# A filter's first layer run as two 64-row tiles of TensorE instead of one 128-row product

## The chip, the cores and the metric

The kernel runs on one core of a Trainium2 chip. The time is that of one execution on the device in microseconds (us), from the first to the last instruction and what lies around them; less is better. One execution was also profiled: its span, its instructions and their waits are what the rows further down are taken from.

## The reference

A long convolution with a filter made by a small network is multiplied into the input, and its result goes through a soft mixture of experts. The change touches only the filter:

```python
def _attn_ref(x, v, pos_emb, w1, w2):          # x, v: (4, 11456, 128); pos_emb: (11456, 64)
    h_mlp = np.maximum(pos_emb @ w1, 0.0) @ w2  # w1: (64, 64), w2: (64, 128)
    window = np.exp(-0.01 * pos)[:, None]
    h_filt = h_mlp * window
    u = x * v
    ...                                         # y: causal convolution of u with h_filt
    return x * y

def _moe_ref(x, phi, w1, w2):
    ...                                         # softmax over tokens and over 32 slots, 8 experts
```

All numbers are 32-bit floats.

## The kernel before

The convolution is done by Fourier transforms of 197 x 111 points that are written as matrix products. The 11,456 positions are indexed by j (99 values, the partitions of most tiles here) and r (56 values, called rows here). Positions 111 j + r and 111 j - r are kept side by side, one for each sign: `pos` holds for each of the 56 rows a block of 128 x 99, in which partitions 0 to 63 are the 64 features of the positions of one sign and partitions 64 to 127 those of the other.

The program starts with the filter's first layer, `hid_step` and `hid_scale`. For each row r, one product (line L150) has the 128 x 99 block of `pos` as the stationary operand and `w1r[:, r]` as the moving one. `w1` is fed as a 128 x 128 matrix with the 64 x 64 weights in two diagonal blocks and zeros elsewhere, so that the 128 columns that come out are the 64 hidden units of the one sign and the 64 of the other. The factor of the window that depends on r is multiplied into `w1` ahead of the product: `w1r[:, r]` is a scaled copy of all 128 columns, made on ScalarE (`scale_one`, L120) for some rows and on POOL (`scale_many`, L123) for the others, three steps ahead. A 32-bit product is two instruction records of TensorE, each with a weight load (PEld) and a stream of the columns (PE).

The rows go in ten steps: 4, then five times 8, then 4, 4, 2 and 2. They are numbered 0 to 9 here, so step 0 is rows 0 to 3, step 1 rows 4 to 11, and step 5 rows 36 to 43. For a step, TensorE writes the products to a PSUM tile `ph` (four buffers), ScalarE writes the positive part of one sign to `hb` (L153), and two operations of VectorE (L155) take the positive part of the other sign and write sum and difference to `hid`. Before the first step eight products on zeros keep TensorE at work (`idle_products`, L117), and four more follow the last.

`pos` is loaded on SyncE's queue in pieces of 4, 4 and six times 8 rows (L288), behind them the inputs x and v of the convolution and the table W. Then follow, on TensorE, the first transform of `hid` (`filter_first`, L196), the second, which reads W (`filter_second`, L208), the first transform of the input (L174), and further on the filter's last layer (`filter_last`, L218: two products side by side in row halves 0 to 63 and 64 to 127) with the long middle part. VectorE prepares x and v meanwhile (L268 to L274). The order on each engine is the order in which the program is written (`inorder`).

Two other places serve as measures below. L707, in the part on experts, transposes 64 x 128 blocks in two row halves with 64 columns streamed. L886 is a single product there that streams one column.

Of the kernel before, what the change touches and what calls it, by code (L numbers as in the profile page):

```python
# [11 lines left out]
F32 = mybir.dt.float32  # L12
F32R = mybir.dt.float32r
AF = mybir.ActivationFunctionType
ALU = mybir.AluOpType
AX = mybir.AxisListType

B, S, D = 4, 11456, 128
# [3 lines left out]
J = 99  # L22
# [3 lines left out]
R = 56  # L26
RP = 64
FO = 64
# [20 lines left out]
@with_exitstack  # L49
def conv_gate_moe(ctx: ExitStack, tc: tile.TileContext, xf, vf, xi, xe, pos, w1, w2, win,  # L50
                  t1x, t1h, wt, t3, t4, phi, mw1, mw2, rep, out):
    nc = tc.nc
    dram = ctx.enter_context(tc.tile_pool(name="dram", bufs=1, space=bass.MemoryType.DRAM))
    hs = dram.tile([G - 1, HP, J, 2 * CG], F32, tag="hs", name="hs")
    scr = dram.tile([D * TOK], F32, tag="scr", name="scr")
    cp = ctx.enter_context(tc.tile_pool(name="cp", bufs=1))
    moe = Moe(tc, cp, scr, phi, mw1, mw2, rep, out)
    moe.ctx = ctx
    with ExitStack() as cctx:
        conv_part(cctx, tc, cp, moe, xf, vf, xi, xe, pos, w1, w2, win, t1x, t1h, wt, t3, t4, hs, scr)  # L60
    next(moe.steps, None)


def conv_part(ctx, tc, cp, moe, xf, vf, xi, xe, pos, w1, w2, win, t1x, t1h, wt, t3, t4, hs, scr):
    nc = tc.nc
# [3 lines left out]
    psh = hid_ps.enter_context(tc.tile_pool(name="psh", bufs=4, space=bass.MemoryType.PSUM))  # L69
# [9 lines left out]
    Tall = cp.tile([128, (B + 1) * 2 * CG * J], F32, tag="T", name="T")  # L79
# [4 lines left out]
    inorder = tc.keep_in_program_order  # L84
# [7 lines left out]
    hid = moe.E[:J, : 2 * RP * FO].rearrange("p (s r f) -> p s r f", s=2, r=RP)  # L92
# [4 lines left out]
    ring = moe.E[:, J * N1 : J * N1 + 2 * HK * 2 * D]  # L97
    ring = ring.rearrange("p (t g k x) -> p t g k x", t=2, g=G, k=HK)
    small = moe.E[:, J * N1 + 2 * HK * 2 * D :]
    w1s = small[:, : 2 * FO]  # L100
    w2s = small[:, 2 * FO : 2 * FO + D]
    wins = small[:, 2 * FO + D :][:, :R]
    tab1h = small[:J, 2 * FO + D + R :][:, : 4 * J]
    w1r = Tall[:, : R * 2 * FO].rearrange("p (r x) -> p r x", r=R)
    pt = W.rearrange("p k n -> p (k n)")[:, J * (N1 - R) :].rearrange("p (r j) -> p r j", r=R)
    spare = [moe.E[:, 4 * C * R + PW * i :][:, :PW] for i in range(2)]

    HR = 8
# [12 lines left out]

    def scale_many(r0, r1):
        inorder(nc.gpsimd.tensor_tensor(  # L123
            out=w1r[:, r0:r1], in0=w1s.unsqueeze(1).to_broadcast([128, r1 - r0, 2 * FO]), op=ALU.mult,
            in1=wins[:, r0:r1].unsqueeze(2).to_broadcast([128, r1 - r0, 2 * FO])))

    def hid_scale(i):
        r0, n = steps[i]
        if i == 0:
            for r in range(1, n):  # L130
                scale_one(r)
        elif i == 1:
            scale_many(r0, r0 + 4)
            for r in range(r0 + 4, r0 + n):
                scale_one(r)
        else:
            if n == HR:
                for r in range(r0 + n - 2, r0 + n):
                    scale_one(r)
                n -= 2  # L140
            if n == 2:
                scale_one(r0 + 1)
                n = 1
            scale_many(r0, r0 + n)

    def hid_step(r0, n):
        ph = psh.tile([J, HR, 2, FO], F32, tag="ph", name=f"ph_{r0}")
        for k in range(n):
            r = r0 + k
            inorder(nc.tensor.matmul(ph[:, k].rearrange("p h f -> p (h f)"), lhsT=pt[:, r],  # L150
                                     rhs=w1r[:, r] if r else w1s, start=True, stop=True))
        hb = ld.tile([J, HR, FO], F32, tag="lv", name=f"hb_{r0}", bufs=2)
        inorder(nc.scalar.activation(hb[:, :n], ph[:, :n, 0], AF.Relu))  # L153
        for s, op in enumerate((ALU.add, ALU.subtract)):
            inorder(nc.vector.scalar_tensor_tensor(out=hid[:, s, r0 : r0 + n], in0=ph[:, :n, 1], scalar=0.0,  # L155
                                                   op0=ALU.max, op1=op, in1=hb[:, :n]))

    def banks(g, u, name, large):
# [127 lines left out]
    for i, n in enumerate(loads):  # L286
        r0 = sum(loads[:i])
# [4 lines left out]
    for i, (r0, n) in enumerate(steps):  # L292
        hid_step(r0, n)
        if i + 3 < len(steps):
            hid_scale(i + 3)
# [878 lines left out]
    return dict(rep=rep, t1x=t1x, t1h=t1h, wt=wt, t3=t3, t4=t4, win=win)  # L1174


def _twice(a):
    o = np.zeros((2, a.shape[0], 2, a.shape[1]), a.dtype)
    o[0, :, 0] = o[1, :, 1] = a
    return o.reshape(2 * a.shape[0], -1)  # L1180


def _index(base):
    j = np.arange(-(JT // 2), JT // 2 + 1) if base else np.arange(J)
    r = np.arange(R)
    p = N1 * j[:, None] + r[None] + base
    b = N1 * j[:, None] - r[None] + base
    m = -N1 * j[:, None] - r[None] + base
    return p, b, m
# [99 lines left out]
```

## Time and profile before

| | |
|---|---|
| median of 3 runs | 890.41 us (890.39 to 890.75) |
| span of the profiled execution | 888.78 us |
| TensorE busy in that span | 858.3 us, 97% |
| first layer's products | 4.64 to 18.16 us |
| next layer's first product | 19.45 us |

The profiled execution is one execution, and its span runs from its first to its last instruction. Engines are PE (TensorE's products), PEld (its weight loads), DVE (VectorE), ACT (ScalarE), POOL (GpSimd) and SP (SyncE, which here only issues transfers). An arrow in brackets names the engine, tile and line whose end released the instruction after an idle time; "issue" there means that the profile shows nothing the engine waited for.

### The profile page before, as it was taken

To read this page: it belongs to the slowest core of one execution; us is meant where nothing else is said; L and a number is where in the kernel's file an instruction comes from. 1 tells how busy PE (TensorE), PEld (TensorE's weight loads), DVE (VectorE), ACT (ScalarE), POOL (GpSimd) and SP (SyncE) were. 2 spreads that over 40 slices of the span, in tenths; PEclk is the share of its full clock that TensorE was granted. 3 is DMA by queue.
4 is the path that set the end of the run, shared out by engine and by line. 5 is a ranking of instruction groups with operands and counts; after the bars stand their busy time and mean duration, and the time that the engine had idled before them with its cause. 6 is when DMAs were issued, how large, how long until landed. Compare 5 with 4: busy or idle time off the path is not lost. (4 is left out here: it accounts for less than half of the span.)

```text
span 888.8 us, 37282 instructions
## 1 busy us (share of the span) xinstructions
PE 858.3 (97%) x16192; PEld 792.5 (89%) x16192; DVE 714.9 (80%) x1239; ACT 455.9 (51%) x971; POOL 393.3 (44%) x538
## 2 busy tenths in 40 slices
PE   9999999999999999999999999999999999999991
PEld 9998989999999999999999999999999997666540
DVE  5967976898899889988988998899779148886791
ACT  5775558315811751473167128414821637887761
POOL 5003860492088029405910960393079013785750
PEclk9999999999999999999999999999999999999996
DMA  9963685548647755775386476557715979993698
GB/s 329 396 193 117 205 249 148 157 147 269 203 125 210 234 165 141 227 235 167 110 282 201 123 224 207 167 167 238 224 57 166 264 182 374 412 369 121 278 417 364
DMA packets 94386, 197.01 MB, mean 222 GB/s; under 512 B 14330, under 2 KB 55708, under 8 KB 90383
## 3 DMA queue, kind: packets, MB, share of 16 engines
q1 hardware_dynamic: 94046, 194.50, 66.8%
q8 instruction: 127, 2.08, 0.9%
q14 instruction: 37, 0.30, 0.1%
q10 hardware_dynamic: 144, 0.07, 0.0%
q0 software_dynamic: 32, 0.07, 0.0%
HBM read 137.73 MB, written 56.86 MB: 219 GB/s over the span
## 5 line engine op out<-in xcount | busy, mean ns | idle before, releaser
L350 POOL TENSOR_TENSOR T<-m 111x256 f32<-111x256 f32 (+1 forms) x199 | 150.8, 758 | 344.5 <-DVE m L344 344.5
L344 DVE TENSOR_TENSOR m<-p,T 111x1024 f32<-111x1024 f32 (+1 forms) x175 | 200.4, 1206 | 14.4 <-PE p L340 7.0
L360 PE MATMUL p<-tab,T 111*99 111x112 f32 x2048 | 205.4, 260 | 1.5 <-POOL T L351 0.3
L360 PEld LDWEIGHTS p<-tab,T 111*99 111x99 f32 x2048 | 198.8, 170 | 6.5 <-issue 1.6
L340 PE MATMUL p<-T,W 128*64 128x128 f32 (+1 forms) x3168 | 196.7, 276 | 0.4 <-issue 0.3
L420 ACT ACTIVATE vc<-p 128x416 f32<-128x416 f32 x112 | 51.9, 516 | 266.2 <-PE p L411 226.6
L340 PEld LDWEIGHTS p<-T,W 128*64 128x64 f32 (+1 forms) x3168 | 181.8, 127 | 2.7 <-issue 0.9
L411 PE MATMUL p<-tab,E 99*64 99x104 f32 x3584 | 174.1, 252 | 1.1 <-DVE E L373 0.6
L411 PEld LDWEIGHTS p<-tab,E 99*64 99x64 f32 x3584 | 166.4, 136 | 3.1 <-ACT vc L420 0.8
L375 ACT ACTIVATE E<-p 99x448 f32<-99x448 f32 x254 | 132.2, 577 | 63.7 <-PE p L360 57.5
L351 POOL TENSOR_TENSOR T<-m 111x256 f32<-111x256 f32 (+1 forms) x199 | 147.4, 740 | 0.0
L186 ACT ACTIVATE T<-p 128x396 f32<-128x396 f32 x240 | 100.4, 539 | 11.5 <-PE p L174 11.4
L174 PE MATMUL p<-tab1x,x 53*64 53x99 f32 x3648 | 86.7, 246 | 0.2 <-ACT E L224 0.2
L174 PEld LDWEIGHTS p<-tab1x,x 53*64 53x64 f32 x3648 | 79.8, 132 | 4.4 <-ACT E L224 0.4
L436 DVE TENSOR_TENSOR p<-p,vc 128x832 f32<-128x832 f32 x46 | 47.3, 1028 | 10.3 <-ACT vc L420 10.3
L268 DVE TENSOR_TENSOR x<-x,T 128x448 f32<-128x448 f32 x51 | 31.6, 619 | 22.2 <-PE p L174 11.2
L274 DVE TENSOR_TENSOR x<-T 128x224 f32<-128x224 f32 x102 | 39.2, 426 | 1.8
L270 DVE TENSOR_TENSOR T<-x 128x224 f32<-128x224 f32 x102 | 39.2, 425 | 1.7
L224 ACT ACTIVATE E<-fl 111x512 f32<-111x512 f32 (+1 forms) x50 | 26.9, 629 | 21.3 <-PE fl L218 21.3
L444 DVE TENSOR_TENSOR E<-p,E 128x824 f32<-128x824 f32 x36 | 36.6, 1017 | 1.2
L713 ACT ACTIVATE xreg<-pt 128x512 f32<-128x512 f32 (+1 forms) x68 | 35.0, 612 | 0.8 <-PE pt L707 0.7
L344 DVE TENSOR_TENSOR m<-p,E 111x1024 f32<-111x1024 f32 (+1 forms) x25 | 28.7, 1202 | 5.1 <-PE p L340 4.9
(156 smaller groups left out, 972.8 us busy)
## 6 DMA issues: line engine op xcount, KB each, us to landing
x<-in_xf_dram SPq DMA_DIRECT2D x114, 256.0 KB, 4.2
out_dram<-xreg SPq DMA_DIRECT2D x16, 1024.0 KB, 10.5
E<-in_xi_dram SPq DMA_DIRECT2D x37, 412.0 KB, 4.0
T<-in_vf_dram SPq DMA_DIRECT2D x65, 224.0 KB, 5.0
scr<-E SPq DMA_DIRECT2D x67, 206.0 KB, 3.7
T<-hs SPq DMA_DIRECT2D x63, 154.0 KB, 4.5
hs<-E SPq DMA_DIRECT2D x12, 784.0 KB, 4.6
mv<-in_vf_dram SPq DMA_DIRECT2D x42, 224.0 KB, 5.2
```

The source lines that it names most:

```text
L174: inorder(nc.tensor.matmul(ps[h][RP * d : RP * d + RP, i, s, :], lhsT=sd[js, i, s, d, :], rhs=tab1x[js, J * (s + d) : J * (s + d + 1)], st ...
L186: inorder(nc.scalar.activation(dst, src, AF.Copy))
L270: inorder(eng.tensor_tensor(out=vt[:, :, m : m + 2], in0=xr[:, :, 0:2], in1=xr[:, :, 2:4], op=op))
L340: inorder(nc.tensor.matmul(ps[ns, i].rearrange("p b c -> p (b c)"), lhsT=W[:, k0 + i, ns], rhs=Tf[:, :, k0 + i, :], start=True, stop=True, ...
L344: inorder(nc.vector.tensor_mul(m[:, :n].rearrange("p k s e c i -> p k s (e c i)").rearrange("p k s (b c) -> p k s b c", c=CG), ps[:, :n].u ...
L350: inorder(eng.tensor_tensor(out=Ty[:, 0], in0=m[:, :n, 0, 0], in1=m[:, :n, 1, 1], op=ALU.subtract))
L351: inorder(eng.tensor_tensor(out=Ty[:, 1], in0=m[:, :n, 1, 0], in1=m[:, :n, 0, 1], op=ALU.add))
L360: inorder(nc.tensor.matmul(pk[:, i, 2 * s : 2 * s + 2, :].rearrange("p q r -> p (q r)"), lhsT=T[0:N1, s, 2 * k + i, u // 2, :, u % 2], rhs ...
L375: inorder(nc.scalar.activation(dst, src, AF.Copy))
L411: inorder(nc.tensor.matmul(pv[RP * h : RP * h + RP, 2 * k + i, w, :], lhsT=E[:J, r, 2 - 2 * w + s, :], rhs=tab4[:, s, o : o + NJ], start=( ...
L420: inorder(nc.scalar.activation(vc[:, w], pv[:, :, 0, :], AF.Copy, scale=2.0 * w - 1.0))
L436: inorder(nc.vector.tensor_tensor(out=pw, in0=pw[:, 1:2].to_broadcast([128, 2, 4, NJ]), in1=vc, op=ALU.add))
```

## The change

`w1` is fed as two copies of the 64 x 64 weights, one above the other (128 x 64), instead of the two diagonal blocks. Each row's product becomes two, one for each sign: 64 rows of the array each, at tile positions (0, 0) and (64, 0), with 99 columns loaded and 64 streamed. The scaled copies have 64 columns instead of 128. In the PSUM tile the sign is now the outer index, so that each sign fills a half of the tile of its own.

```diff
-    w1s = small[:, : 2 * FO]
+    w1s = small[:, :FO]
...
-    w1r = Tall[:, : R * 2 * FO].rearrange("p (r x) -> p r x", r=R)
+    w1r = Tall[:, : R * FO].rearrange("p (r x) -> p r x", r=R)
...
     def scale_many(r0, r1):
         inorder(nc.gpsimd.tensor_tensor(
-            out=w1r[:, r0:r1], in0=w1s.unsqueeze(1).to_broadcast([128, r1 - r0, 2 * FO]), op=ALU.mult,
-            in1=wins[:, r0:r1].unsqueeze(2).to_broadcast([128, r1 - r0, 2 * FO])))
+            out=w1r[:, r0:r1], in0=w1s.unsqueeze(1).to_broadcast([128, r1 - r0, FO]), op=ALU.mult,
+            in1=wins[:, r0:r1].unsqueeze(2).to_broadcast([128, r1 - r0, FO])))
...
     def hid_step(r0, n):
-        ph = psh.tile([J, HR, 2, FO], F32, tag="ph", name=f"ph_{r0}")
+        ph = psh.tile([J, 2, HR, FO], F32, tag="ph", name=f"ph_{r0}")
         for k in range(n):
             r = r0 + k
-            inorder(nc.tensor.matmul(ph[:, k].rearrange("p h f -> p (h f)"), lhsT=pt[:, r],
-                                     rhs=w1r[:, r] if r else w1s, start=True, stop=True))
+            for s in range(2):
+                fs = slice(FO * s, FO * s + FO)
+                inorder(nc.tensor.matmul(ph[:, s, k], lhsT=pt[fs, r], rhs=w1r[fs, r] if r else w1s[fs],
+                                         start=True, stop=True, tile_position=(FO * s, 0)))
         hb = ld.tile([J, HR, FO], F32, tag="lv", name=f"hb_{r0}", bufs=2)
-        inorder(nc.scalar.activation(hb[:, :n], ph[:, :n, 0], AF.Relu))
+        inorder(nc.scalar.activation(hb[:, :n], ph[:, 0, :n], AF.Relu))
         for s, op in enumerate((ALU.add, ALU.subtract)):
-            inorder(nc.vector.scalar_tensor_tensor(out=hid[:, s, r0 : r0 + n], in0=ph[:, :n, 1], scalar=0.0,
+            inorder(nc.vector.scalar_tensor_tensor(out=hid[:, s, r0 : r0 + n], in0=ph[:, 1, :n], scalar=0.0,
...
-... w1=_twice(inputs["w1"]), ...
+... w1=np.concatenate([inputs["w1"], inputs["w1"]], 0), ...
```

On TensorE, at the program's start, the row of instructions before is this; ph_113 is step 0, and the shape is partitions by columns of the result.

```order
L117 MATMUL idle<-E 128x128 x8
L150 MATMUL ph_113<-E,W 99x128
L150 MATMUL ph_113<-T,W 99x128 x3
L150 MATMUL ph_125<-T,W 99x128 x8
L150 MATMUL ph_141<-T,W 99x128 x8
L150 MATMUL ph_157<-T,W 99x128 x8
```

With the change the same place on TensorE reads so.

```order
L117 MATMUL idle<-E 128x128 x8
L152 MATMUL ph_113<-E,W 99x64 x2
L152 MATMUL ph_113<-T,W 99x64 x6
L152 MATMUL ph_129<-T,W 99x64 x16
L152 MATMUL ph_153<-T,W 99x64 x16
L152 MATMUL ph_177<-T,W 99x64 x16
```

There are twice as many products with half the columns, in the same steps; nothing else stands between them, and no instruction has changed its place.

On ScalarE, from the table load to the third hb, the program with the change reads so; the copies are L120, and the hb operations are now L155.

```order
L282 ACTIVATE T<-E 99x2
L120 ACTIVATE T<-E 128x64 x9
L155 ACTIVATE hb_122<-ph_113 99x256
L120 ACTIVATE T<-E 128x64 x2
L155 ACTIVATE hb_146<-ph_129 99x512
L120 ACTIVATE T<-E 128x64 x2
L155 ACTIVATE hb_170<-ph_153 99x512
```

Before, the same rows stood in the same order with copies of 128x128; nothing moved, only the copies' width is halved. VectorE's and SyncE's rows are the same in both.

## Rows read from the trace of the kernel before

**Rows 1.** The page: busy us of each engine, share of the span, instructions.

```profile
PE 858.3 (97%) x16192; PEld 792.5 (89%) x16192; DVE 714.9 (80%) x1239; ACT 455.9 (51%) x971; POOL 393.3 (44%) x538
```

**Rows 2.** Windows: stretch, its length, busy us per engine, clock, DMA share, GB/s.

```profile
4.43:18.13 13.70, 13.70 (x114) 13.35 (x113) 7.98 (x15) 7.66 (x21) 7.98 (x8) 1.00 1.03 370
```

**Rows 3.** Timeline of VectorE, first layer: start, us, what, count, idle before it.

```profile
9.03 1.29 DVE L155 SCALAR_TENSOR_TENSOR E<-ph,hb 99x512 f32<-99x512 f32 x2 [1.26 <-ACT hb L153]
10.82 1.29 DVE L155 SCALAR_TENSOR_TENSOR E<-ph,hb 99x512 f32<-99x512 f32 x2 [0.51 <-ACT hb L153]
...
16.06 3.53 DVE L155 SCALAR_TENSOR_TENSOR E<-ph,hb 99x512 f32<-99x512 f32 x10 [0.46 <-ACT hb L153]
```

**Rows 4.** Timeline of ScalarE, first layer.

```profile
8.40 0.60 ACT L153 ACTIVATE hb<-ph 99x512 f32<-99x512 f32 x1 [0.84 <-PE ph L150]
...
13.69 0.60 ACT L153 ACTIVATE hb<-ph 99x512 f32<-99x512 f32 x1 [1.15 <-PE ph L150]
```

**Rows 5.** Timeline of TensorE's products, 0 to 45 us.

```profile
1.06 3.79 PE L117 MATMUL idle<-E 99*128 99x128 f32 x16 [1.06 <-DVE E L279]
4.64 0.63 PE L150 MATMUL ph<-E,W 128*99 128x128 f32 x2
...
19.45 22.24 PE L196 MATMUL f<-E 99*64 99x198 f32 x256 [0.16 <-DVE E L155]
```

**Rows 6.** Timeline of TensorE's products that start from 4 to 7 us.

```profile
5.07 2.20 PE L150 MATMUL ph<-T,W 128*99 128x128 f32 x12
```

**Rows 7.** Window of 8 to 12 us, first layer's products alone.

```profile
8.00:12.00 4.00, 4.00 (x39) 1.00 1.04 378
```

**Rows 8.** Line L150: ns of one, min/median/max, first and last start, form.

```profile
L150 PE MATMUL ph<-T,W x110: 272/273/421, 5.1 to 17.9; 128*99 128x128 f32 x110
```

**Rows 9.** Window of 740.4 to 741.2 us, transposes of L707 alone.

```profile
740.40:741.20 0.80, 0.80 (x30) 0.80 (x30) 1.00 1.10 446
```

**Rows 10.** Groups by form, TensorE: busy us, mean ns of one, idle before.

```profile
L707 PE MATMUL pt<-aux,ffw 64*128 64x64 f32 x320 | 12.9, 226 | 1.4 <-issue 1.4
```

**Rows 11.** Timeline of TensorE's products, 75 to 80 us.

```profile
75.45 2.00 PE L218 MATMUL fl<-E 64*111 64x128 f32 x32
```

**Rows 12.** Groups by form, TensorE's weight loads: busy us, mean ns, idle.

```profile
L360 PEld LDWEIGHTS p<-tab,T 111*99 111x99 f32 x2048 | 198.8, 170 | 6.5 <-issue 1.6 <-POOL T L351 0.8 <-ACT E L375 0.4
...
L865 PEld LDWEIGHTS pa<-xreg,ev 128*32 128x32 f32 x492 | 13.1, 110 | 0.7
...
L707 PEld LDWEIGHTS pt<-aux,ffw 64*128 64x128 f32 x320 | 11.1, 139 | 5.4 <-ACT xreg L713 3.4 <-issue 1.6
...
L886 PEld LDWEIGHTS pmt<-xreg,aux 128*128 128x128 f32 x2 | 0.3, 188 | 0.2 <-issue 0.2
```

**Rows 13.** Timeline of TensorE's weight loads, 814.3 to 815 us.

```profile
814.47 0.30 PEld L886 LDWEIGHTS pmt<-xreg,aux 128*128 128x128 f32 x2 [0.20 <-issue]
```

**Rows 14.** Groups by form, 0 to 20 us: busy us, mean ns, idle.

```profile
L155 DVE SCALAR_TENSOR_TENSOR E<-ph,hb 99x512 f32<-99x512 f32 x10 | 6.4, 687 | 3.1 <-ACT hb L153 3.1
L123 POOL TENSOR_TENSOR T<-E 128x768 f32<-128x768 f32 x4 | 5.8, 1468 | 0.0
L120 ACT ACTIVATE T<-E 128x128 f32<-128x128 f32 x17 | 5.6, 391 | 0.2 <-DMA E<-in_w_dram 0.2
```

**Rows 15.** Timeline of SyncE's DMA issues, 0 to 6 us.

```profile
1.19 3.98 SPq L288 DMA_DIRECT2D W<-in_pos_dram  x8
```

**Rows 16.** DMA issues, third and eighth load of pos: KB, us to landing.

```profile
W<-in_pos_dram SPq DMA_DIRECT2D x1, 396.0 KB, 4.4
W<-in_pos_dram SPq DMA_DIRECT2D x1, 396.0 KB, 7.5
```

**Rows 17.** DMA issues of 17 to 42 us: KB each, median us to landing.

```profile
W<-in_wt_dram SPq DMA_DIRECT2D x11, 499.5 KB, 6.9
```

**Rows 18.** Timeline of VectorE, 60 to 64 us.

```profile
62.55 1.85 DVE L188 COPY T<-p 128x396 f32<-128x396 f32 x3 [5.26 <-PE p L174]
```

**Rows 19.** Timeline of TensorE's products, 61 to 76 us.

```profile
73.92 1.60 PE L174 MATMUL p<-tab1x,mv 53*64 53x99 f32 x63 [1.27 <-issue]
```

More of the change, by code (lines that the diff above doesn't have):

```diff
@@ L99, in conv_part @@
     small = moe.E[:, J * N1 + 2 * HK * 2 * D :]
-    w1s = small[:, : 2 * FO]
-    w2s = small[:, 2 * FO : 2 * FO + D]
-    wins = small[:, 2 * FO + D :][:, :R]
-    tab1h = small[:J, 2 * FO + D + R :][:, : 4 * J]
-    w1r = Tall[:, : R * 2 * FO].rearrange("p (r x) -> p r x", r=R)
+    w1s = small[:, :FO]
+    w2s = small[:, FO : FO + D]
+    wins = small[:, FO + D :][:, :R]
+    tab1h = small[:J, FO + D + R :][:, : 4 * J]
+    w1r = Tall[:, : R * FO].rearrange("p (r x) -> p r x", r=R)
     pt = W.rearrange("p k n -> p (k n)")[:, J * (N1 - R) :].rearrange("p (r j) -> p r j", r=R)
@@ L1174, in _constants @@
     return dict(rep=rep, t1x=t1x, t1h=t1h, wt=wt, t3=t3, t4=t4, win=win)
[L1177 to L1180, printed above, removed]
 def _index(base):
@@ L1268 @@
     k = _constants()
-    feeds = dict(xf=xf, vf=vf, xi=xi, xe=xe, pos=pe, w1=_twice(inputs["w1"]), w2=np.concatenate([inputs["w2"], inputs["w2"]], 0), win=k["win"],
+    feeds = dict(xf=xf, vf=vf, xi=xi, xe=xe, pos=pe, w1=np.concatenate([inputs["w1"], inputs["w1"]], 0), w2=np.concatenate([inputs["w2"], inputs["w2"]], 0), win=k["win"],
                  t1x=k["t1x"], t1h=k["t1h"], wt=k["wt"], t3=k["t3"], t4=k["t4"],
```

## The prediction

> **What bounds the kernel now.** Begin with the page's busy times: TensorE is busy for 97% of the span [rows 1], so a place where TensorE gets through sooner can move everything behind it. Next the windows by stage. The change lies in one stage, the filter's first layer, from 4.43 to 18.13 us: TensorE is busy in all of it, VectorE and ScalarE for under 60%, and the DMA engines are full [rows 2]. Then the timelines of the two engines that follow TensorE there. VectorE takes each step's pair of operations in 1.29 us and then idles half a microsecond for ScalarE's hb; only from 16.06 does it run through without a gap [rows 3]. ScalarE's hb waits for the products [rows 4]. So TensorE sets the pace until about 16 us, and VectorE's tail sets the end: from the first operation of step 5 (rows 36 to 43) at 16.06 to the first product of the next layer at 19.45 [rows 3, 5] pass 3.39 us.
>
> TensorE's own pace shows two levels. A product here is two records, so the 56 products are 112. The first start 0.21 us apart (two in the 0.43 us from 4.64 to 5.07 [rows 5]); twelve start between 5.07 and 7.00 [rows 6], which fits seven intervals of 0.213 and four of 0.109, so the pace doubles at 6.56 us. From then on 39 records of 0.27 us touch a stretch of 4.00 us [rows 7, 8]: (4.00 + 0.27)/39 = 0.109 us each. TensorE had then been at work without a pause since 1.06 us [rows 5], for 5.5 us. [...] The 24th record, the last of rows 0 to 11, starts at 6.56 + 14 x 0.109 = 8.09, and hb of step 1 at 8.40 [rows 4], 0.31 later.
>
> **The change, part by part.** Each product over 128 rows and 128 columns becomes two over 64 rows and 64 columns, side by side in the array. So the 112 records become 112 pairs, and what counts is the pace p of a pair against 0.109.
>
> No row has a pair of this shape (load 64x99, stream 64 columns), so I bound p. The fastest near row is the transposes: two 64-row tiles, 128 columns loaded, 64 streamed, 30 records (15 pairs) of 0.226 us touching 0.80 us [rows 9, 10]: p = 1.03/15 = 0.068. The slowest is the filter's last layer, two 64-row tiles that load 111 and stream 128 columns: 16 pairs in 2.00 us [rows 11], less 0.27 for the last record: 1.73/15 = 0.115. In between, the weight load speaks. Its length grows with columns: 110 ns for 32, 170 for 99, 188 for 128 [rows 12], some 0.81 ns a column. Where a product streams one column and nothing else can set the pace, two loads of 128 columns take 0.30 us together [rows 13], so the second starts 0.30 - 0.19 = 0.11 after the first: for 99 columns 0.11 x 99/128 = 0.085. Two loads in different row halves do not queue: a pair of the last layer loads 2 x 111 columns in 0.115, where one after the other would take 0.19. I take p = 0.085, because the load still covers 99 columns while the stream is halved; the transposes move data unchanged, and their loads are shorter (139 ns for 128 columns against 188 [rows 12]), so their row stands further off. At the lower level I double it, 0.170.
>
> [...]
>
> Now the sum. The first pair starts at 4.64 as before, since the idle products ahead do not change. Rows 0 to 3 are 8 pairs: 4.64 + 1.36 = 6.00. Until 6.56, 3.3 more pairs pass; the other 4.7 of rows 4 to 7 take 0.40, to 6.96; the last pair of rows 8 to 11 starts at 6.96 + 7 x 0.085 = 7.56. Then hb at 7.87 and VectorE's step 1 at 7.87 + 0.63 = 8.50, where it stood at 9.03 [rows 3, 4]. Each further step of 8 rows is 16 pairs, 1.36 us; VectorE without gaps needs about 1.21 (two operations end 1.29 after the first starts [rows 3], one is 0.69 long [rows 14], so each follows 0.60 after the one before). So TensorE still sets the pace, barely: step 5 starts on VectorE at 8.50 + 4 x 1.36 = 13.94, and the next layer at 13.94 + 3.39 = **17.33 instead of 19.45: 2.1 us sooner**.
>
> Edits that cost nothing here. The scaled copies of w1 halve: 17 on ScalarE (0.39 us each) and nine on POOL (up to 1.47 us) [rows 14], made some steps ahead of their use; without that cover a step would wait half of one such operation less, 0.2 to 0.7 us. hb and VectorE's operations keep their sizes. The two signs' sums change places in PSUM, with the same elements per operation. w1's load halves; the first product waits for the idle products anyway. The eight loads of pos are issued about half a microsecond apart from 1.19 on [rows 15]; the third, issued at 2.1, lands 4.4 us later, at 6.5, ahead of 6.96, and the last, issued at 4.7, 7.5 us later, at 12.2 [rows 16], when its first row is due at about 13.8.
>
> What is late next? The next layer streams for 22.24 us [rows 5] on a table whose load stands on the queue right behind pos. All eleven pieces of W are issued by 42 us and land 6.9 us later [rows 17]; the layer that reads them starts after the 22.24 us and needs the last piece only near its end. VectorE, which prepares the convolution's inputs meanwhile, idles 5.26 us for TensorE before 62.55 [rows 18], so it can take 2.1 us less without holding TensorE up. From there on each transfer is released by work that moves along.
>
> The profiled execution spans 888.78 us, so 886.7 is the new span. The median of the runs, 890.41, lies 1.63 above the span; with the same distance the time is **888.3 us**.
>
> **The rivals.**
> - *The loads show* (slower). If a tile's next load did not hide behind that tile's stream, p would be 0.085 + 0.055 = 0.14. Step 1 would reach VectorE at 9.76, the last pair would start at 21.1 and the next layer near 22.2: 2.7 us later, **893.1 us**. If the two halves' loads queued as well it would be 0.17 and 896.4. It decides from p = 0.109 up. The full array speaks against it: its record comes every 0.109 although load and stream would make 0.19 together. [...]
> - *VectorE becomes the bound.* With the transposes' p of 0.068, step 1 reaches VectorE at 8.10, then a step takes its 1.21 us: the next layer starts at 16.3, 3.1 us sooner: **887.3 us**.
> - *The higher clock level comes late.* In the load-bound pairs the array streams for only part of the time. If the level rose as long after 4.64 as it did after 1.06, at 10.1, 23 pairs would pass at 0.170, row 43 would be done at 14.8, and the next layer start near 19.0: **890.0 us**. For it: nothing in this trace shows such pairs at the lower level.
> - *The pace lies between the load and the last layer's row* (0.090 to 0.115): a gain of 1.7 down to a loss of 0.6 us, **888.7 to 891.0**.
> - *The time is given back.* The transfers are full through this stage [rows 2], and TensorE idles for neither engine nor transfer at 73.92 (1.27 us, "issue" [rows 19]); the change adds 224 TensorE instructions, and if such stalls or a late W take the gain: **890.4 us**. Against it: the slack above.
>
> **How the numbers follow.** Forecast 0.56, with its own range from 887.5 to 888.7 (p from 0.07 to 0.09); VectorE as bound 0.12; clock late 0.11; slow pace 0.09; given back 0.07; loads show 0.05. What this measurement can tell from no change is about 0.2%, 1.8 us, a gain that p = 0.089 would just give. Most of the forecast and the second rival are faster: 0.60; slower is the first rival and a little of the rest: 0.07; the remaining 0.33 is the same. From 887.0 to 890.8 lies all but about one case in ten.
>
> **What would show it.** Right: pairs of the new shape about 0.085 us apart after the level rises; VectorE's step 1 near 8.5 and its idle gaps before each step shrunk from 0.5 to 0.1 or 0.2 us; the next layer's first product near 17.3; the distance from there to the end unchanged at 869.3 us. Wrong at the pace: pairs at 0.11 or more, ScalarE's hb still a full step behind. Wrong at the level: records of the lower level's length past 7 us. Wrong behind: the layers after 17.3 wait for W or for instructions, and the distance to the end grows.

## The result, and the profile after

The change makes the kernel slower: 898.63 us median of 4 runs (897.70 to 900.08), against 890.58 us (890.39 to 894.67, 4 runs) before, a ratio of 1.0082 with an interval of 1.0063 to 1.0102. The profiled execution of the changed kernel took 899.40 us and spans 897.6, that of before 888.8.

The page's line on busy times for the kernel after; it answers to [rows 1].

```profile
PE 868.9 (97%) x16304; PEld 801.0 (89%) x16304; DVE 714.9 (80%) x1239; ACT 454.9 (51%) x971; POOL 389.2 (43%) x538
```

TensorE alone is busy for longer: its products by 10.6 us, its loads by 8.5. Its timeline says where (start, us, what, count); it answers to [rows 5].

```profile
1.06 3.78 PE L117 MATMUL idle<-E 99*128 99x128 f32 x16 [1.06 <-DVE E L281]
4.77 0.60 PE L152 MATMUL ph<-E,W 64*99 64x64 f32 x4
5.16 18.54 PE L152 MATMUL ph<-T,W 64*99 64x64 f32 x220
23.64 2.07 PE L117 MATMUL idle<-E 99*128 99x128 f32 x8
25.64 24.66 PE L198 MATMUL f<-E 99*64 99x198 f32 x256
50.90 19.22 PE L210 MATMUL f<-W,T 128*64 128x111 f32 x396 [0.60 <-ACT T L201]
```

The next layer's first product starts at 25.64 us instead of 19.45, 6.2 later. That layer itself takes 24.66 us instead of 22.24, 2.4 more. The one behind it starts at 50.90 instead of 42.29 (19.45 + 22.24 + the same 0.60), 8.6 later. From there to the end are 846.7 us, and were 846.5. So 8.6 of the 8.8 us between the two spans arise in these two stages, and next to nothing comes back or goes lost behind them. The row of that layer in the kernel before:

```profile
42.29 19.22 PE L208 MATMUL f<-W,T 128*64 128x111 f32 x396 [0.60 <-ACT T L199]
```

TensorE is not waiting there. The windows of the kernel after (columns as in [rows 2]), the first of which answers to [rows 2]:

```profile
4.77:23.64 18.87, 18.87 (x226) 18.75 (x225) 8.62 (x17) 6.56 (x19) 3.46 (x7) 1.00 1.03 372
25.64:50.90 25.26, 24.66 (x257) 22.97 (x257) 24.40 (x64) 16.66 (x32) 0.00 (x0) 1.00 0.96 348
26.00:31.00 5.00, 5.00 (x32) 3.65 (x32) 4.86 (x13) 1.56 (x3) 0.00 (x0) 1.00 0.69 221
31.00:36.00 5.00, 5.00 (x61) 4.97 (x59) 4.79 (x14) 3.66 (x7) 0.00 (x0) 1.00 1.03 387
```

Products and loads fill the first layer's stage, and no row of TensorE there names an idle time. But the next layer passes 32 records from 26 to 31 us, and 61 in the five microseconds after. The pace doubles at 31 us; in the kernel before it doubled at 6.56. The clock column reads 1.00 in all of these stretches, as it did before [rows 2, 7], so only the records tell the level; a granted clock of 0.50 at the lower one is shown further down, by the run with four tiles. Here are those of line L152 (ns of one as min/median/max, first and last start, form), which answer to [rows 8]:

```profile
L152 PEld LDWEIGHTS ph<-T,W x220: 287/287/287, 5.1 to 23.2; 64*99 64x99 f32 x110
L152 PE MATMUL ph<-T,W x220: 371/371/371, 5.2 to 23.3; 64*99 64x64 f32 x110
```

From the first to the last, all 220 products have one length, and all 220 loads. In the kernel before, the products had two, 272 and 421 ns. Whether 371 ns is the length of the lower or of the higher level, the first experiment shows: the same instructions take 248 ns there. They follow each other (18.54 - 0.37)/219 = 0.083 us apart, so a pair comes every 0.166 us.

VectorE and ScalarE wait for this pace. VectorE's timeline of the kernel after answers to [rows 3]:

```profile
9.72 1.29 DVE L157 SCALAR_TENSOR_TENSOR E<-ph,hb 99x512 f32<-99x512 f32 x2 [2.12 <-ACT hb L155]
12.43 1.29 DVE L157 SCALAR_TENSOR_TENSOR E<-ph,hb 99x512 f32<-99x512 f32 x2 [1.43 <-ACT hb L155]
...
20.43 1.95 DVE L157 SCALAR_TENSOR_TENSOR E<-ph,hb 99x512 f32<-99x512 f32 x4 [1.38 <-ACT hb L155]
22.88 1.72 DVE L157 SCALAR_TENSOR_TENSOR E<-ph,hb 99x256 f32<-99x256 f32 x6 [0.50 <-ACT hb L155]
```

ScalarE's timeline of the kernel after answers to [rows 4]:

```profile
9.09 0.60 ACT L155 ACTIVATE hb<-ph 99x512 f32<-99x512 f32 x1 [1.81 <-PE ph L152]
...
17.14 0.60 ACT L155 ACTIVATE hb<-ph 99x512 f32<-99x512 f32 x1 [2.07 <-PE ph L152]
```

VectorE idles 1.4 us ahead of steps 2 to 5, where it was 0.5; step 5 reaches it at 20.43 instead of 16.06. Its last operation of the layer ends at 24.60 (22.88 + 1.72), yet the next layer starts at 25.64: the four closing idle products, 2.07 us long at the lower level, have come onto the path as well, for 1.0 us.

### The profile page after: what moved, and what is told of

It reads as the page before. It is cut to its first block, busy times and chain, and to the rows that moved or that the text cites. A ratio compares the mean times of both kernels' runs of the same rounds, so it can differ in the third digit from the quotient of the medians.

```text
span 897.6 us, 37506 instructions
## 1 busy us (share of the span) xinstructions
PE 868.9 (97%) x16304; PEld 801.0 (89%) x16304; DVE 714.9 (80%) x1239; ACT 454.9 (51%) x971; POOL 389.2 (43%) x538
## 5 line engine op out<-in xcount | busy, mean ns | idle before, releaser
L1123 PE MATMUL pw<-cs,so 32*128 32x512 f32 (+2 forms) x192 | 32.9, 633 | 0.7 <-DVE xreg L1130 0.7
```

Of the source, the lines that this page charges most:

```text
L1123: inorder(nc.tensor.matmul(po[:, :na].rearrange("p k t -> p (k t)"), lhsT=so[NSLOT * a : NSLOT * a + NSLOT], rhs=ct[NSLOT * a : NSLOT * a ...
```

## The experiments

The theory after this result (A) was that the stream of pairs has the predicted pace at either level, and that only the level of TensorE's clock differs: it did not rise while the pairs ran. The rivals: the pairs are slow in themselves, whatever the level; or it is the row tiling, not the load-bound stream, that keeps the level down (R).

### Idle products doubled

```diff
-    idle_products(8)
+    idle_products(16)
```

> The changed kernel with 16 idle products ahead of the first layer instead of 8, so that TensorE is at the higher clock level before the first pair of row tiles. Theory A (the 64-column pairs cannot bring the level up, since each waits for its 99-column load, but they keep a level that is up): idle products end near 7.2 us, pairs come every 0.083 us, next layer starts near 18.8, time about 889.8 us. Rival B (the pairs also let a risen level fall): pairs return to 0.167 us in the stage and the time is 897 us or more. Rival C (the lower level was not the cause of the loss, the pairs are slow as such): pairs at 0.167 us although full-array products ahead of them reached 0.109, about 901 us.

Measured: 891.79 us (890.02 to 893.40, 10 runs) against 891.69 for before in the same session (890.12 to 894.43, 20 runs); ratio 0.9995, interval 0.9981 to 1.0009. TensorE's timeline of this kernel:

```profile
1.06 6.26 PE L117 MATMUL idle<-E 99*128 99x128 f32 x32 [1.06 <-DVE E L281]
7.25 0.39 PE L152 MATMUL ph<-E,W 64*99 64x64 f32 x4
7.48 9.44 PE L152 MATMUL ph<-T,W 64*99 64x64 f32 x212
...
19.27 22.23 PE L198 MATMUL f<-E 99*64 99x198 f32 x256 [0.15 <-DVE E L157]
```

And its line L152, as read above:

```profile
L152 PEld LDWEIGHTS ph<-T,W x220: 158/164/164, 7.4 to 17.6; 64*99 64x99 f32 x110
L152 PE MATMUL ph<-T,W x220: 247/248/296, 7.5 to 17.6; 64*99 64x64 f32 x110
```

The pairs are the same instructions; they start 2.5 us later, with the level already up, and take 248 ns instead of 371, every (9.44 - 0.25)/211 x 2 = 0.087 us a pair. The next layer starts at 19.27, 6.4 us sooner than in the changed kernel, although its first layer began 2.5 us later, and takes 22.23 us again. With that theory A stands against slow pairs, and the loss is accounted for; nor did the pairs let the risen level fall in this profile (the expectation's rival B). The time is that of before, 2.0 us above the expected 889.8. The eight idle products more take up nearly all that the pairs bring in this stage (19.27 against 19.45 before), and from there to the end this execution took 870.6 us, where the one of before took 869.3.

VectorE's and ScalarE's timelines of this kernel show that TensorE still sets the pace, barely:

```profile
11.69 7.72 DVE L157 SCALAR_TENSOR_TENSOR E<-ph,hb 99x512 f32<-99x512 f32 x16 [0.16 <-ACT hb L155]
...
13.87 0.60 ACT L155 ACTIVATE hb<-ph 99x512 f32<-99x512 f32 x1 [0.80 <-PE ph L152]
15.27 0.60 ACT L155 ACTIVATE hb<-ph 99x512 f32<-99x512 f32 x1 [0.80 <-PE ph L152]
```

VectorE's row names no gap from 11.69 on, but only because the gaps are short: of the 5.41 us from 11.69 to 17.10 it is busy for 5.07, so it idles 0.11 us ahead of each of steps 3 to 5. ScalarE's hb waits 0.80 us for the products and comes every 1.40 us, which is 16 pairs of 0.087.

### Full-array products first, pairs from row 12 on

This is the kernel before with the pairs in rows 12 to 55 alone; they take the diagonal blocks of the wide copies, so the copies are not halved.

```diff
+    FULL_ROWS = 12
...
+        full = r0 < FULL_ROWS
...
+            if full:
+                inorder(nc.tensor.matmul(ph[:, k].rearrange("p h f -> p (h f)"), lhsT=pt[:, r],
+                                         rhs=w1r[:, r] if r else w1s, start=True, stop=True))
+                continue
+            for s in range(2):
+                fs = slice(FO * s, FO * s + FO)
+                inorder(nc.tensor.matmul(ph[:, s, k], lhsT=pt[fs, r], rhs=w1r[fs, r, fs],
+                                         start=True, stop=True, tile_position=(FO * s, 0)))
```

> Rows 0 to 11 as full-array products on the block-diagonal w1 as before the change, rows 12 to 55 as two row tiles that take their 64 columns from the same 128-column copies. Theory A: the level rises near 6.5 us as in the kernel before, the pairs then come every 0.083 us, VectorE's steps every 1.33 us instead of 1.75, next layer near 17.8 instead of 19.45: 888.7 us. Rival B (the pairs let the level fall): 895 us or more. Rival C (pairs slow as such): pairs at 0.167, next layer near 23.5, about 894.5 us.

Measured: 889.62 us (887.26 to 891.05, 9 runs) against the same 891.69; ratio 0.9968, interval 0.9954 to 0.9982: faster. TensorE's timeline of this kernel:

```profile
5.06 3.85 PE L158 MATMUL ph<-T,W 128*99 128x128 f32 x22
8.84 7.57 PE L163 MATMUL ph<-T,W 64*99 64x64 f32 x168
...
18.77 22.23 PE L209 MATMUL f<-E 99*64 99x198 f32 x256
```

The pairs run 0.088 us apart ((7.57 - 0.25)/167 x 2) and the next layer starts 0.7 us sooner than before, at 18.77. The expected 17.8 was missed by 1.0. The level rose later than in the kernel before: the 22 records start within 3.58 us (3.85 - 0.27), which fits about 12.4 intervals of 0.213 us and 8.6 of 0.109, so it rose near 7.7 instead of 6.56. That is about 0.6 of the 1.0; the pace of 0.088 instead of 0.083 makes the other 0.4 over 88 pairs.

### No row tiles, products cut into two of 64 columns

This takes the row tiling out of the change and leaves the stream: in the kernel before, each product becomes two over the same 128 x 99 load, with 64 columns each.

```diff
+            for h in range(2):
+                fs = slice(FO * h, FO * h + FO)
+                inorder(nc.tensor.matmul(ph[:, k, h], lhsT=pt[:, r], rhs=w1r[:, r, fs] if r else w1s[:, fs],
+                                         start=True, stop=True))
```

> The kernel before with each product cut in two by columns: the whole array loads the same 128x99 block twice and streams 64 columns each time, no row tiles. Theory A (the load-bound pace with pauses between streams keeps the level low, tiles or not): records every 0.167 us through the stage, 224 of them, next layer near 43 us, about 916 us. Rival R (it is the row tiling as such that keeps the level low): the level rises near 6.5 us, records every 0.083, next layer near 25.6, about 896.6 us.

Measured: four executions of 896.39, 915.89, 918.43 and 918.64 us against 891.69; two groups so far apart that no ratio is given. The profiled one is that of 915.89 (span 914.1). Its TensorE timeline:

```profile
5.24 36.87 PE L152 MATMUL ph<-T,W 128*99 128x64 f32 x220
...
43.86 23.97 PE L198 MATMUL f<-E 99*64 99x198 f32 x256
```

And its line L152:

```profile
L152 PE MATMUL ph<-T,W x220: 374/374/375, 5.2 to 41.7; 128*99 128x64 f32 x110
```

Here each of the 220 records comes (36.87 - 0.37)/219 = 0.167 us after the one before, twice the 0.083 of the changed kernel's records, which fits that both halves load over the same rows. All have one length, so the level stays down through all 36.9 us, with no row tile in this layer; pace, next layer and time are those that theory A expected (0.167, 43 and 916 us). So rival R is wrong for this execution: the level stayed down in such a stream without row tiles too. The one execution at 896.39 lies 20 us below the others, about half of those 36.9 us. It is also where rival R expected the time with the level up (896.6). That its level was up is only argued, since it has no profile.

### Four tiles of 64 x 64

The changed kernel with each pair's products also cut by columns of the array, into 64 and 35 positions, so that a load has no more columns than its stream.

```diff
+                for h in range(2):
+                    js = slice(RP * h, min(RP * h + RP, J))
+                    inorder(nc.tensor.matmul(ph[js, s, k], lhsT=pt[fs, r, js], rhs=w1r[fs, r] if r else w1s[fs],
+                                             start=True, stop=True, tile_position=(FO * s, RP * h)))
```

> The changed kernel with each 99-column product cut into two column tiles as well (64 and 35 columns), four tiles of 64x64, so that a load covers at most 64 columns and the array streams nearly all the time. Theory A: the level rises near 6.5 us; groups of four every 0.06 us unless TensorE's instructions come too slowly (four times as many as before the change); 887.5 to 890 us. Rival R (row tiling as such keeps the level low): groups every 0.112 us throughout, the level still low in the next layer, 891.5 us or more.

Measured: 897.56 us (895.47 to 900.57, 6 runs); ratio 1.0072, interval 1.0049 to 1.0095. TensorE's timeline of this kernel:

```profile
5.00 4.14 PE L154 MATMUL ph<-T,W 64*35 64x64 f32 x197
13.19 3.46 PE L154 MATMUL ph<-T,W 64*64 64x64 f32 x127 [4.05 <-issue]
19.19 2.02 PE L154 MATMUL ph<-T,W 64*64 64x64 f32 x100 [2.54 <-issue]
```

A window of line L154 alone (columns: stretch, length, PE, PEld, clock, DMA share, GB/s):

```profile
7.00:8.50 1.50, 1.50 (x118) 1.50 (x111) 1.00 1.02 410
```

Windows of all engines (columns as in [rows 2]; the one before the DMA share is the clock):

```profile
9.00:13.00 4.00, 0.14 (x9) 0.01 (x2) 1.62 (x3) 0.60 (x3) 0.00 (x0) 1.00 1.04 352
13.50:16.90 3.40, 3.16 (x121) 2.97 (x113) 1.96 (x4) 1.19 (x2) 0.00 (x0) 0.50 1.07 386
17.00:20.30 3.30, 1.11 (x76) 1.11 (x79) 0.51 (x1) 0.49 (x1) 0.00 (x0) 1.00 1.05 384
20.40:30.50 10.10, 9.21 (x89) 6.92 (x82) 9.81 (x26) 3.22 (x10) 0.00 (x0) 0.50 0.76 260
31.00:36.00 5.00, 5.00 (x62) 5.00 (x62) 4.83 (x14) 3.90 (x8) 0.00 (x0) 1.00 1.03 399
```

At first the tiles do what was wanted. From 5.00 to 6.50 us 64 records of 0.31 us come at about 0.11 us a group of four ((1.50 + 0.31)/64 x 4), from 7.00 to 8.50 118 records of 0.22 us at 0.058. So the level rose between 6.5 and 7.0 us, while row tiles ran, which again speaks against R. The 0.058 also bears on what sets a pair's pace: 64 columns are streamed as before, so the stream does not need the 0.087. Loaded are 64 columns at most instead of 99, and the pace falls about as they do (0.058/0.087 = 0.67, 64/99 = 0.65). Then TensorE stands still for 4.05 us and later for 2.54, for no engine and no transfer that the profile shows. Behind the first stop the granted clock is 0.50 (13.50 to 16.90 us); from 17.00 to 20.30, most of it the second stop, it reads 1.00, and from 20.40 to 30.50 again 0.50 (over the whole execution it is 0.982 to 0.985 in all six, against 0.989 to 0.991 in the changed kernel's four). The layer behind runs at the lower level until some time between 30.5 and 31 us. So theory A's time (887.5 to 890) was missed by more than 7 us. Whether it was the shorter load that let the level rise is not shown: with 4 full rows, further down, it also rose in a stream with 99 columns loaded. The stops come with the doubled count of instructions; that TensorE lacks instructions there fits the "issue", but no run here shows it by itself.

### How few full rows are enough, and how many are too many

The second experiment again with 4 and with 20 full rows, and once more with 12, all in another session (before: 890.83 us, 889.42 to 895.09, 29 runs).

```diff
-    FULL_ROWS = 12
+    FULL_ROWS = 4     # then 20, then 12 again
```

> As the mix of full-array products and row tiles, but only rows 0 to 3 as full-array products, which end near 6.4 us; the level rose at 6.5 us in the profile of before and at 7.7 in that of the mix with 12 rows, so the pairs begin before it. Theory A (the pairs cannot bring the level up): pairs every 0.167 us in most executions, next layer near 25 us, 896 to 899 us, with single executions near 888 where the level came earlier. Rival D (the pairs only delay the rise by a few us): next layer near 19 to 21 us, 889 to 893 us in all.

Measured with 4 full rows: 889.11 us median, nine of ten executions from 887.14 to 891.87, one at 899.73; ratio 0.9991, interval 0.9965 to 1.0016. Windows of line L163, the pairs alone (columns: stretch, length, PE, PEld, clock, DMA share, GB/s):

```profile
6.50:7.40 0.90, 0.89 (x11) 0.89 (x12) 1.00 1.00 387
7.60:11.60 4.00, 4.00 (x96) 4.00 (x92) 1.00 1.03 387
```

And of TensorE's timeline the next layer:

```profile
18.40 22.24 PE L209 MATMUL f<-E 99*64 99x198 f32 x256
```

The first pair starts at 6.51. Eleven records from there to 7.40 are 0.16 us a pair, the lower level's pace; 96 records of 0.25 us touch the second window, (4.00 + 0.25)/96 x 2 = 0.089 us a pair. So the pairs began at the lower level and it rose about 1.1 us later, near 7.6, and the next layer starts at 18.40, 1.05 us sooner than before. Theory A in its strict form, that pairs cannot bring the level up, expected most executions near the changed kernel's time; nine of ten are not, and in the profiled one the level rose while pairs ran. So a stream of pairs that begins at the lower level does not always stay there. Whether the pairs themselves brought the level up is not shown: full-array products had run until 1.1 us before, and in the eight other executions under 892 us, which have no profile, the level may have been up ahead of the first pair. Rival D's next layer at 19 to 21 us did not come out either.

The execution at 899.73 has the changed kernel's time, but not its clock. Over the whole execution its granted clock is 0.978, where the other nine read 0.989 to 0.992 and the four of the changed kernel 0.989 to 0.991, although the changed kernel's profile shows the lower level up to 31 us. The column counted nothing there: it read 1.00 from 26 to 31 us too. By an estimate from these numbers 2 x 0.022 x 897.9 = 39.5 us of the late execution were recorded at the lower level (0.5), and 14 to 20 us of each of the others. So in it, unlike in the changed kernel, some 20 us more were counted as low, which points to a level that had been up and fell again. Where is not known, since this execution has no profile. That pairs always keep a risen level is therefore not shown.

> The mix with rows 0 to 19 as full-array products. Theory A: eight rows fewer at 0.083 x 2 instead of 0.109 x 2 us, so step 2 reaches VectorE some 0.4 us later and the time is 0.4 us above the mix with 12 rows run beside it, still under the kernel before by about 1.3 to 1.6 us. Rival E (the mix with 12 rows sometimes loses the level before it is up for good, and 20 rows guard against that): as fast as or faster than 12 rows, with less spread.

Measured with 20 full rows: 892.15 us (889.45 to 894.38, 10 runs); ratio 1.0012, interval 0.9995 to 1.0028. TensorE's timeline of this kernel:

```profile
8.36 2.83 PE L158 MATMUL ph<-T,W 128*99 128x128 f32 x24 [0.31 <-DMA W<-in_pos_dram]
...
19.65 22.25 PE L209 MATMUL f<-E 99*64 99x198 f32 x256 [0.16 <-DVE E L168]
```

Of the 21 executions with 12 rows in both sessions the slowest took 891.05, so there was no late one that more full rows could guard against, and with 20 the pairs' gain is gone. The expected 0.4 us above 12 rows came out as 3.9 (888.25, below). The profiles place 0.7 of that in this stage (19.65 against 18.94), 0.31 of it a wait for the third load of `pos`; the rest is not located.

> The mix with rows 0 to 11 as full-array products once more, with more rounds. Theory A: 1.7 to 2.1 us under the kernel before (ratio 0.9976 to 0.9981), all executions under those of the change. Rival (the first measurement was chance): no difference from before.

Measured with 12 full rows: 888.25 us (886.07 to 890.02, 12 runs); ratio 0.9967, interval 0.9955 to 0.9979. TensorE's timeline of this kernel:

```profile
5.06 2.23 PE L158 MATMUL ph<-T,W 128*99 128x128 f32 x14
8.00 1.09 PE L158 MATMUL ph<-T,W 128*99 128x128 f32 x8 [0.71 <-DMA W<-in_pos_dram]
9.01 7.56 PE L163 MATMUL ph<-T,W 64*99 64x64 f32 x168
...
18.94 22.24 PE L209 MATMUL f<-E 99*64 99x198 f32 x256
```

The gain of the first session repeats, even with a wait of 0.71 us for `pos` in the profile. This version beats both kernels. Of its 2.6 us (890.83 less 888.25) the profile places 0.5 in this stage (18.94 against 19.45); the rest is not located, since the profiled execution, at 889.65 us, is one of its slower ones.

## Why the prediction was wrong

**The step that failed** is "Until 6.56, 3.3 more pairs pass": the sum let the level rise at the time at which it rose in the kernel before, although from 4.64 us on TensorE now did other work. It rose at 31 us. Nor is 6.56 fixed for the same work: with full-array products first, the rows put the rise near 7.7 in the first profile with 12 full rows, and near 6.2 in the second (13 intervals in 2.23 - 0.27 = 1.96 us, about 5.2 of 0.213 and 7.8 of 0.109). The changed kernel's pairs, from 4.77 on, begin ahead of all of these. The pairs took 0.166 us each to the end, and VectorE's step 1 stood at 9.72 instead of the predicted 8.50, step 5 at 20.43 instead of 13.94, and the next layer at 25.64 instead of 17.33.

**The pace was right at both levels.** 0.166 us was measured at the lower level, where 0.170 was taken, and 0.087 at the higher (first experiment), where 0.085 was. So "the loads show" was wrong. The 0.055 that it adds for a tile's stream is half of 0.109, 64 columns for 128, an estimate; no run shows that term, and the pairs came every 0.087 us. The pace went with the columns loaded (0.087 with 99 of them, 0.058 with at most 64 in the four tiles) and not with those streamed, 64 in both. The 0.166 at the lower level is 1.9 times the 0.087.

**The rest of the sum was right where the level is up.** With the pace of 0.085 from the first pair on, the predicted stage of 12.69 us (4.64 to 17.33) shrinks by 11.3 x 0.085 = 0.96 to 11.73. The first experiment took 12.02 (7.25 to 19.27), with 1.40 us a step instead of 1.36. VectorE idled 0.11 us ahead of its steps there, within the predicted 0.1 or 0.2, so TensorE set the pace as barely as the sum had it.

**The edits costed at nothing were hidden**: TensorE names no idle time from 4.77 to 23.64, so neither the copies nor `pos` held it up. The margin for `pos` was thin, though: the sum let the third load land at 6.5 us and needed it at 6.96, and in the last two experiments' profiles TensorE waited for it until 8.36 and 8.00. What is behind the filter's second transform kept its distance to the end (846.7 against 846.5 us). The step "the distance from there to the end unchanged at 869.3" failed for the next layer alone, which ran its first 5.4 us at the lower level and took 2.4 us more.

**The rival that came true** is "the higher clock level comes late", with a chance of 0.11. That the level comes late was right; the size was far off. It let the level rise at 10.1 us, as long after the pairs' start as the full products had needed, and priced that at 890.0. (Its 23 pairs at 0.170 should read 32, which is 5.46/0.170; the 14.8 and the 890.0 go with 32.) The case in which the level does not rise while the pairs run could have been worked out from the same numbers: 112 x 0.170 = 19.0 us of pairs, to 23.7, and a next layer some microseconds late even if it ran at full level. With it the range would have reached to about 895 (23.7 is 4.2 us behind 19.45), and the forecast's own chance would have been smaller.

**What stays open** is what exactly decides when the level rises. It stayed down through a whole stream that began at the lower level in the changed kernel (all 220 records 371 ns) and in the profiled execution with halves (374 to 375 ns). It rose within such a stream in the profile with four full rows ahead (near 7.6 us), and within one of shorter loads in that with four tiles (between 6.5 and 7.0 us). Where the stream began at the higher level, it stayed there in every profile (16 idle products, 12 and 20 full rows: 0.087 to 0.088 us a pair); the one late execution with four full rows, by its granted clock of 0.978, probably lost a level that had been up. What decides a single execution no run here shows.

## What to carry to other kernels

Before replacing long products at a program's start by more and shorter ones, ask at which clock level they will run, and price the case in which the level of the kernel before is not reached at all; here that case cost 8 us (898.63 against 890.58) where the forecast gain was 2. Read the level from the length of records of one form, not from the clock's column alone: here 371 ns and 248 ns both stood beside 1.00. And look for a stage's loss in the next layer too, which here lost 2.4 us more. If the shorter products pay at all, let the longer ones run first: with 12 full rows ahead, the same pairs brought 0.3% here.

## What was not expected of the hardware

- The level stayed down for 18.5 us of pairs without a pause, and for 36.9 us of products with 64 columns (all records 374 or 375 ns), with no idle time of the engine; in the kernel before it was up after 5.5 us of full-array products. With the same products at the start, it rose near 6.2 us in one profile and near 7.7 in another.
- With four tiles the level had risen by 7.0 us; the granted clock was 0.50 behind the stop of 4.05 us (13.50 to 16.90 us), and 0.50 again from 20.40 to 30.50. At the lower level the clock's column read 1.00 in the changed kernel (4.77 to 31 us) and with 4 full rows (6.50 to 7.40), as it did at the higher.
- TensorE stopped for 4.05 us with nothing shown as waited for, after about 200 records of 64 x 64 tiles had passed in 4.14 us.
- The unchanged kernel spreads from 889.42 to 895.09 us over 29 runs of one session, more than the 2.1 us that the change was forecast to bring; only medians of many runs tell 0.3% apart.
